# Two decayed-attention outputs feed two feed-forward layers: three places in the order of the side work are rewritten

## The chip, the cores and the metric

The kernel runs on one core of one Trainium2 chip. The metric is the device time of one execution in microseconds (us), as the median of three runs. Engines are named as in the profile: PE is TensorE (PEld its weight loads), DVE is VectorE, ACT is ScalarE, POOL is GpSimd, SP is SyncE, which here issues nearly all DMAs.

## The reference, cut to what matters

```python
# q, k, v: (4, 8, 576, 64), f: (4, 8, 576)
scores = q @ k^T / 8 + cumsum(log f)[i] - cumsum(log f)[j]      # causal
attn = softmax(scores);  x = attn @ v                           # x: (2304, 512)
h = x @ w_in;   x = (h * clip(h + 3, 0, 6) / 6) @ w_out         # w_in (512, 2048), w_out (2048, 512)
h = x @ w_in2;  x = (max(h, 0) + alpha * min(h, 0)) @ w_out2    # layer two, same shapes
```

All weights arrive as 64-bit numbers.

## The kernel before, in words

**Attention.** 32 heads in 16 pairs; every pair gives nine units of up to 128 rows. A head's raw data, q and k in one tile `rqk` of 128x1216 words, is requested by `load_head`. `prep_head` and `prep_low` (lines 296 to 317) make the two operands of the score product of it, and the decay's cumulated sums come in as four extra rows of each operand (`q2[64:68]`, `k2[64:68]`). For heads 0 and 1 these rows are built on the core. For all others they are written to DRAM once, as `ak_d` (line 502) and `aq_d` (line 517), and read back head by head (lines 295 and 296). The first unit of head 2 multiplies `k2` on line 347. Head 3's raw data is requested at line 518, behind both row stores; SP issues in program order.

**Feed-forward.** Tokens are three pairs p of 2 x 384, hidden features eight groups g of 256. A set (layer, g, p) multiplies a 2x2 block of the token pair with a 2x2 block of the group in seven products instead of eight (`product`, `PROD`), each of 2 x 3 matmuls, since an operand is kept as a rounded high part and a low part (the rest): high x high, high x x-low, weight-low x high. `SEQ` is the order of a set: products 1, 5, 6, 3, 7, 2, 4 (P1 to P7 in the text), with a `q` between them, one piece of the output product of the set before (`piece`). P1, P6, P7 and P4 accumulate in one bank hA, P5 and P3 in hC, P2 alone in hB; after P1, P6 and P5 ACT copies the bank away (`keep`, line 687), and after P3, P7 and P2 DVE adds the copy (`add`, line 690). P6 must not write hA before P1's copy is done, P7 not before P6's copy, P4 not before P7's sum, P3 not hC before P5's copy. `activate` makes g of each sum on ACT and DVE, then ACT rounds it (line 664) and POOL makes its low part (line 665). The first three pieces of the next set need the g of P7 first, and its low part with their third matmul.

**Slots.** Every character of `SEQ` is a slot. Work that is not PE's is hung on slots: `at` for what follows a product, `behind` for side work, and the table of numbers beside each name says in which slot it is written into its engine's stream. Engines run their streams in that order.

**Weights (side work).** `conv_ops` turns the raw words of a group into single precision: magnitude m (ACT), floor f, shift s, join j, sign g (DVE), for the four pieces 0 to 3 (0 and 1 are w_in). Out of pieces 0 (tile `wa`) and 1 (`wb`) POOL forms S1, S2 (in `wc`), S3 (in `wa`) and S4 (in `wb`), line 162. ACT then rounds the parts a, b, c, d (ha, hb, hc, hd, line 176), and POOL makes the low parts (la, lb, lc, ld, line 180). Part a holds the weights of P1 and P7 and is made of S3's tile `wa`, b those of P2 and P4, c those of P5 and P6 (tile `wc`), d that of P3, made of S4. In layer two a conversion for g+1 starts three slots into set (g, p=0) and is needed at set (g+1, p=0), 26 slots after that set's start; there are seven. `CONV_EVEN` is the table of these seven and of nothing else. m2 (the magnitude of piece 2) writes `wc` again, which S4 reads.

**Token blocks (side work).** `build_parts` forms the seven x blocks of a pair: sums (line 223), high parts on ACT (line 226), low parts (line 231) on POOL or DVE in turn. P1, P5, P6, P3, P7, P2, P4 use blocks 0, 3, 6, 2, 4, 1, 5. `build` with `even` spreads the list of `BUILD` in the order of its text evenly over slots: for pair 1 in layer one, from slot 1 of set (0, g=1, p=0) with 1.5 steps a slot, and for pair 0 of layer two, in a stretch of 51 slots in layer one's last third.

The lines that the steps touch:

```python
PROD = {1: (0, 0, "A"), 2: (2, 1, "B"), 6: (5, 6, "A"), 5: (4, 3, "C"), 7: (1, 4, "A"), 3: (6, 2, "C"),
        4: (3, 5, "A")}
SEQ = ("1qq5q6q3q7q2q4q", "1q5q6q3q7q2q4")
FIRST = ("152637..4", "15qq6qq3q7q2q4q", "1qq5qq6qq3q7q2q4q")
SUM = {"S1": (("S", 0), (0, 1), (1, 1), ALU.add), "S3": ((0, 1), (0, 0), (0, 1), ALU.subtract),
       "S2": (("S", 1), ("S", 0), (0, 0), ALU.subtract), "S4": ((1, 0), (1, 0), ("S", 1), ALU.subtract)}
```

Of the kernel before, what the change touches and what calls it, by code (L numbers as in the profile page):

```python
# [21 lines left out]
def decay_attention_ffn2_kernel(ctx, tc, qk, v, f, wi1, wo1, wi2, wo2, alpha, out):  # L22
# [24 lines left out]
    CONV_FIRST = "ho0 2 m3 2 lo0 3 f3 3 s3 4 j3 5 g3 6 ho1 8 lo1 9 wi0 30 wi1 33 wo0 36 wo1 38"  # L47
    CONV_A = "m0 0 f0 2 s0 3 j0 4 g0 5 m1 4 f1 6 s1 7 j1 8 g1 9"
    CONV_B = "hb 11 S1 11 S3 12 lb 13 S2 13 S4 14 ha 14 hc 16 la 16 hd 17 lc 18 ld 19 m2 19 f2 20 s2 21 j2 22 g2 23 m3 21 f3 24 s3 25 j3 26 g3 27 ho0 25 lo0 27 ho1 29 lo1 31 wi0 40 wi1 43 wo0 46 wo1 48"
    CONV_EVEN = "m0 0 f0 1 s0 2.5 j0 4 g0 5.5 m1 5 f1 7 s1 8.5 j1 10 g1 11.5 S1 12 S2 13 hc 14 S3 14 hb 15 lc 15 lb 16 ha 16 S4 17 m2 18 hd 18 f2 19 ld 19 s2 20 la 20 j2 21 m3 21 g2 22.5 f3 23 ho0 23 lo0 24 s3 24.5 j3 26 g3 27 ho1 28 lo1 29 wi0 40 wi1 43 wo0 46 wo1 48"  # L50
    CONV_TURN = "S1 11 S3 12 S2 13 hb 30 ha 30 hc 31 lb 32 la 33 S4 34 lc 35 m2 38 hd 37 ld 38 f2 41 s2 42 j2 43 g2 44 m3 42 f3 46 s3 47 j3 48 g3 49 ho0 47 lo0 49 ho1 51 lo1 52 wi0 58 wi1 61 wo0 64 wo1 66"
    BUILD = "h0 2 l0 4 a3 6 h3 9 l3 11 h2 9 l2 11 a4 13 a6 15 h4 16 l4 18 h1 17 l1 19 h6 19 l6 21 a5 22 h5 26 l5 28"
    early = {}
    ORD, QA, QB, QL = "TMEVDS", 3, 7, 2
# [163 lines left out]
    def build_parts(k, p, add, subs):  # L218

        turn = [0]  # L220

        def combine(d, a, b):
            add.tensor_sub(out=d, in0=a, in1=b)  # L223

        def high(b, c, x):
            nc.scalar.copy(out=XS[k][0][:, b, c], in_=x)  # L226

        def low(b, c, x):
            e = subs[turn[0] % len(subs)]
            turn[0] += 1  # L230
            e.tensor_sub(out=XS[k][1][:, b, c], in0=x, in1=XS[k][0][:, b, c].bitcast(F32))  # L231

        adds, highs, lows = {}, {}, {}
        for c in range(KH):
            b11, b12, b21, b22 = (place(p, j, n, c) for j in range(2) for n in range(2))
            for b, d, x, y in ((3, b11, b12, b11), (4, b12, b22, b12), (6, b22, b22, b11), (5, b21, b21, b22)):
                adds[b, c] = lambda a=(d, x, y): combine(*a)
            for b, x in ((0, b11), (1, b21), (2, b22), (6, b22), (3, b11), (4, b12), (5, b21)):
                highs[b, c] = lambda a=(b, c, x): high(*a)
                lows[b, c] = lambda a=(b, c, x): low(*a)  # L240
        return adds, highs, lows
# [18 lines left out]
    def attention():  # L260
        with ExitStack() as ax:
# [13 lines left out]
            def load_head(h):  # L275
                raw = rawp.tile([128, QW + S], F32, tag="raw", name="rqk")
                nc.sync.dma_start(out=raw, in_=qk[h])
                raws[h] = (raw[:, 0:QW], raw[:, QW:QW + S])
                if h % 2 == 0:
                    p = h // 2  # L280
                    vt = vp.tile([128, KT, 128], F32, tag="v", name="vt")
                    nc.sync.dma_start(out=vt, in_=v[p // NPAIR, p % NPAIR])
                    vs[p] = vt
# [8 lines left out]
            def prep_head(h):  # L292
                if h not in slots:
                    q1, q2, k1, k2 = op_tiles(h)
                    nc.sync.dma_start(out=q2[64:68].bitcast(F32), in_=aq_d[h % 2, h // 2])
                    nc.sync.dma_start(out=k2[64:68].bitcast(F32), in_=ak_d[h % 2, h // 2])
                q1, q2, k1, k2 = slots[h]
                rq, rk = raws[h]
                e = AS0[h] if h < 2 else AS
                scaled(e[0], q1, rq, SCALE)  # L300
                scaled(e[1], k1, rk)
                if h < 4:
                    scaled(e[2], k2[0:64], rk[0:64])
# [196 lines left out]
            load_head(2)  # L500
            for a in range(2):
                nc.sync.dma_start(out=ak_d[a, 0:NP], in_=ak[32 * a:32 * a + NP].bitcast(F32))
            prep_head(1)
            prep_low(1)
            nc.gpsimd.memset(three, 3.0)
# [9 lines left out]
                scaled("P", aq[ps, 0:2, t0:t0 + TAIL], hl[ps, :, 512:S].bitcast(F32))  # L515
            for a in range(2):
                nc.sync.dma_start(out=aq_d[a, 0:NP], in_=aq[32 * a:32 * a + NP].bitcast(F32))
            load_head(3)
            nc.gpsimd.tensor_scalar(out=alpha_sb, in0=alpha_sb, scalar1=-1.0, scalar2=None, op0=ALU.mult)
            px.close()  # L520
            ptp = ax.enter_context(tc.tile_pool(name="ptp", bufs=3, reuse_waits="tile"))
# [111 lines left out]
    def aside(d, fn):  # L633
        behind.setdefault(now[0] + int(d), []).append(fn)
# [104 lines left out]
    def side_work(s):  # L739

        ff, g, p = s

        def conversion(ops, text, keep, scale=1, shift=0, first=0, last=10 ** 6):
            for name, t in table(text, first, last):
                if keep or name[0] != "w":
                    aside(t * scale + shift, ops[name])

        def build(k, pair, subs, add=nc.vector, even=None):
            for i, (t, fn) in enumerate(build_ops(k, pair, add, subs)):
                aside(t if even is None else even[0] + i / even[1], fn)  # L750

        both = (nc.gpsimd, nc.gpsimd, nc.vector)
        if s == (0, 1, 0):
            conversion(early["first"], CONV_FIRST, True)
            build(1, 1, both, even=(1, 1.5))
        if s == (0, 0, 1):
            ops = conv_ops(0, 2)
            conversion(ops, CONV_A, True, 1, 1)
            conversion(ops, CONV_B, True, 1, 4, 0, 25)
            conversion(ops, CONV_B, True, 1, 7, 25)  # L760
        if p == 0 and (1 if ff else 2) <= g + 1 < NG and not (ff == 0 and g < 2):
            ops, keep = conv_ops(ff, g + 1), g + 1 < NG - 2
            for text in ((CONV_EVEN,) if ff else (CONV_A, CONV_B)):
                conversion(ops, text, keep, 1, 3 if ff else 5)
        if p == NPR - 1:
            order = gorder[ff][1]
            j = order.index(g)
            if j >= 2:
                load_w(ff, g, 1)
            if 1 <= j < NG - 1:  # L770
                load_w(ff, order[j + 1], 0)
            if ff == 0 and j == 1:
                build(1, 0, (nc.gpsimd,), nc.gpsimd, (0, 0.7))
            if ff == 0 and j == NG - 3:
# [106 lines left out]
```

## Time and profile before

| | |
|---|---|
| runs | 1023.65, 1024.52, 1025.59 us; median 1024.52 |
| the profiled execution | 1023.57 us, of which the span of instructions is 1021.8 |
| its mean granted clock of PE | 0.992 |
| busy share: DVE, ACT, POOL | 72%, 58%, 58% |
| chain that ended last: PE, DVE, POOL, ACT | 71%, 15%, 5%, 4% |
| DMA moved | 139.18 MB, mean 136 GB/s |

The profile was taken of one execution. In its timeline a row is a start, a duration, the engine, the line and the operation, out<-in, the shape, how many in a row are merged (x), and in brackets how long the engine was idle before it and what released it. A row's duration holds the instruction's own latency, so rows of PE overlap. In the list of waits each row gives an engine and line, what it waited for, the total, how often, and the longest.

### The profile page before, as it was taken

Reading aid. Unit: us, or ns where it says so; the run is one execution under the profiler, and the core shown is the slowest. Engines: PE = TensorE matmul, PEld = TensorE weight load, DVE = VectorE, ACT = ScalarE, POOL = GpSimd, SP = SyncE. Lnnn points to the kernel's source line nnn. Section 1 sums busy time; section 2 is a strip of 40 time slices with the busy share of each in tenths; the row PEclk is TensorE's granted clock in tenths of the full one; section 3 lists DMA queues with packets and bytes.
Section 4 is the critical chain, followed back from the end, with each engine's and each line's share of the span. In section 5 each row is a group of like instructions: output and inputs, shape, how many; then the busy total and the mean of one; then the engine's idle time right before and its main releaser. Section 6 shows DMA issues by size and latency. Waiting matters only on the chain.

```text
span 1021.8 us, 15850 instructions
## 1 busy us (share of the span) xinstructions
PE 966.4 (95%) x5488; PEld 862.7 (84%) x5488; DVE 739.2 (72%) x1284; ACT 588.5 (58%) x1444; POOL 589.0 (58%) x577
## 2 busy tenths in 40 slices
PE   4999999998999999999999997999999999999998
PEld 3666666678899999998999996888888888888987
DVE  6787987857688788878345668677887778735454
ACT  4677787776555555554544354766555556564452
POOL 7467578856655656566555377565556556532221
PEclk9899999999999999999999998999999999999999
DMA  7555576501424444210254513344244420244531
GB/s 206 178 173 153 173 241 212 149 6 42 155 71 169 181 171 181 94 43 1 76 223 179 203 53 104 131 166 175 85 174 163 167 83 0 94 170 160 226 144 73
DMA packets 32260, 139.18 MB, mean 136 GB/s; under 512 B 4156, under 2 KB 4156, under 8 KB 29044
## 3 DMA queue, kind: packets, MB, share of 16 engines
q1 hardware_dynamic: 32176, 138.17, 39.0%
q8 instruction: 43, 0.70, 0.3%
q14 instruction: 37, 0.30, 0.1%
q10 hardware_dynamic: 4, 0.00, 0.0%
HBM read 94.06 MB, written 39.94 MB: 131 GB/s over the span
## 4 chain that ended last, share of the span: by engine, by line
PE 71%; DVE 15%; POOL 5%; ACT 4%; issue 3%; DMA 1%; SPq 1%; ACTq 0%; DVEq 0%; POOLq 0%
PE o L715 17%; PE o L713 16%; PE hA L682 16%; PE hC L682 9%; PE pv L436 4%; PE hB L682 4%; DVE nm L323 3%; PE tp L379 2%; PE sc L346 2%; POOL wi L180 2%; POOL g L665 1%; DVE nm L325 1%; DVE r L223 1%; ACT g L664 1%; PE sc L347 1%
## 5 line engine op out<-in xcount | busy, mean ns | idle before, releaser
L682 PE MATMUL hA<-xh,wi 128*128 128x384 f32 x768 | 227.1, 341 | 22.2 <-POOL wi L180 11.2
L713 PE MATMUL o<-g,wo 128*128 128x384 f32 x1152 | 232.3, 340 | 1.2 <-POOL g L665 1.2
L715 PE MATMUL o<-wo,g 128*128 128x512 f32 x864 | 224.1, 395 | 1.8 <-POOL g L665 1.4
L665 POOL TENSOR_TENSOR g<-t,g 128x384 fp32r<-128x384 f32 x120 | 127.7, 1065 | 162.2 <-ACT g L664 142.5
L713 PEld LDWEIGHTS o<-g,wo 128*128 128x128 f32 x1152 | 205.8, 189 | 2.1 <-POOL g L665 1.8
L715 PEld LDWEIGHTS o<-wo,g 128*128 128x128 f32 x864 | 160.5, 188 | 29.0 <-POOL g L665 2.7
L682 PEld LDWEIGHTS hA<-xh,wi 128*128 128x128 f32 x768 | 142.1, 189 | 29.8 <-POOL wi L180 13.5
L665 POOL TENSOR_TENSOR g<-s,g 128x384 fp32r<-128x384 f32 x72 | 75.8, 1053 | 155.3 <-ACT g L664 144.9
L733 DVE TENSOR_TENSOR r<-o,r 128x512 f32<-128x512 f32 x126 | 86.5, 687 | 64.0 <-PE o L715 62.9
L682 PE MATMUL hA<-xl,wi 128*128 128x384 f32 x384 | 130.4, 340 | 2.1 <-POOL xl L231 2.1
L722 DVE SCALAR_TENSOR_TENSOR r<-o,r 128x384 f32<-128x384 f32 x168 | 91.4, 551 | 50.5 <-PE o L713 50.1
L664 ACT CAST g<-t 128x384 fp32r<-128x384 f32 x120 | 61.7, 514 | 107.4 <-DVE t L656 89.2
L682 PE MATMUL hC<-xh,wi 128*128 128x384 f32 x384 | 114.3, 338 | 1.3 <-ACT s L687 1.3
L331 ACT ACTIVATE p<-sc,nm 128x128 f32<-128x128 f32 (+4 forms) x160 | 84.5, 531 | 21.3 <-DVE nm L325 9.9
L323 DVE TENSOR_REDUCE nm<-sc 128x1 f32<-128x128 f32 (+4 forms) x160 | 71.5, 469 | 10.5 <-PE sc L348 7.8
L231 POOL TENSOR_TENSOR xl<-r,xh 128x384 fp32r<-128x384 f32 x65 | 74.8, 1168 | 5.1 <-ACT xh L226 4.9
L682 PEld LDWEIGHTS hA<-xl,wi 128*128 128x128 f32 x384 | 72.7, 189 | 5.4 <-POOL xl L231 2.3
L664 ACT CAST g<-s 128x384 fp32r<-128x384 f32 x72 | 37.0, 514 | 65.9 <-DVE s L659 65.1
L682 PEld LDWEIGHTS hC<-xh,wi 128*128 128x128 f32 x384 | 71.1, 188 | 3.8 <-ACT s L687 1.6
L687 ACT COPY s<-hA 128x384 f32<-128x384 f32 x96 | 45.9, 478 | 44.3 <-PE hA L682 44.2
L379 PE MATMUL tp<-ident,p 128*128 128x128 f32 x384 | 69.4, 285 | 0.6 <-ACT pt L395 0.6
L346 PE MATMUL sc<-k,q 128*128 128x256 f32 (+2 forms) x128 | 55.9, 437 | 11.6 <-DVE k L314 9.4
(128 smaller groups left out, 1927.2 us busy)
## 6 DMA issues: line engine op xcount, KB each, us to landing
wid<-wi SPq DMA_DIRECT2D x24, 896.0 KB
wi<-wid SPq DMA_DIRECT2D x12, 1792.0 KB
rqk<-in_qk SPq DMA_DIRECT2D x32, 608.0 KB
raw<-in_wi SPq DMA_DIRECT2D x32, 512.0 KB
raw<-in_wo SPq DMA_DIRECT2D x32, 512.0 KB
wod<-wo SPq DMA_DIRECT2D x24, 512.0 KB
wo<-wod SPq DMA_DIRECT2D x12, 1024.0 KB
vt<-in_v SPq DMA_DIRECT2D x16, 320.0 KB
```

Of the source, the lines that this page charges most:

```text
L231: e.tensor_sub(out=XS[k][1][:, b, c], in0=x, in1=XS[k][0][:, b, c].bitcast(F32))
L323: nc.vector.tensor_reduce(out=nm[:, i:i + 1], in_=src, axis=AX.X, op=ALU.max, negate=True)
L331: nc.scalar.activation(out=pt[:, c0:c0 + cw], in_=src, func=AF.Exp, bias=nm[:, 0:1], scale=1.0, accum_out=dsts[i])
L346: nc.tensor.matmul(out=sc[:, 0:n], lhsT=q1[:, qs], rhs=k1[:, 0:n], start=True, stop=False)
L379: nc.tensor.transpose(tp[:, j, :], pt[:, 128 * j:128 * j + 128], ident)
L664: nc.scalar.copy(out=gt[n][i][:, 0], in_=hold["g"])
L665: nc.gpsimd.tensor_sub(out=gt[n][i][:, 1], in0=hold["g"], in1=gt[n][i][:, 0].bitcast(F32))
L682: nc.tensor.matmul(out=h, lhsT=a, rhs=b[:, x, kc], start=new and kc + e == 0, stop=kc == KH - 1 and e == 2, skip_group_check=not new)
L713: nc.tensor.matmul(out=o[:, 0:NB], lhsT=a[:, cs], rhs=b, start=st, stop=sp)
L715: nc.tensor.matmul(out=o, lhsT=b[:, cs], rhs=a, start=st, stop=sp)
L722: later(0, lambda: nc.vector.scalar_tensor_tensor(out=acc, in0=o[:, 0:NB], scalar=1.0 / 6.0, in1=acc, op0=ALU.mult, op1=ALU.add))
L733: nc.vector.tensor_add(out=acc, in0=o, in1=acc)
```

## The change

Three edits. In `CONV_EVEN` part a's rounding and low part move ahead of part b's, and the steps of pieces 0 and 1 and of the sums are written up to 1.5 slots earlier. `build` with `even` takes its order from a new list, `BUILD_FIRST`, in which block 6 (P6's) stands ahead of blocks 4 and 1. `load_head(3)` moves from behind the `aq_d` stores to between the `ak_d` and the `aq_d` stores.

```diff
-    CONV_EVEN = "m0 0 f0 1 s0 2.5 j0 4 g0 5.5 m1 5 f1 7 s1 8.5 j1 10 g1 11.5 S1 12 S2 13 hc 14 S3 14 hb 15 lc 15 lb 16 ha 16 S4 17 m2 18 hd 18 f2 19 ld 19 s2 20 la 20 j2 21 ...
+    CONV_EVEN = "m0 0 f0 1 s0 2 j0 3.5 g0 5 m1 4 f1 6.5 s1 8 j1 9 g1 10 S1 11 S2 12 S3 12 hc 13 ha 13 lc 14 hb 14 la 15 lb 16 S4 17 m2 18 hd 18 f2 19 ld 19 s2 20 j2 21 ...
+    BUILD_FIRST = "h0 l0 a3 h3 l3 h2 l2 a4 a6 h6 l6 h4 l4 h1 l1 a5 h5 l5"
     BUILD = "h0 2 l0 4 a3 6 h3 9 l3 11 h2 9 l2 11 a4 13 a6 15 h4 16 l4 18 h1 17 l1 19 h6 19 l6 21 a5 22 h5 26 l5 28"
...
-    def build_ops(k, p, add, subs):
+    def build_ops(k, p, add, subs, even=None):
         adds, highs, lows = build_parts(k, p, add, subs)
+        if even is not None:
+            fns = [{"h": highs, "l": lows, "a": adds}[name[0]][int(name[1]), c]
+                   for name in BUILD_FIRST.split() for c in range(KH)]
+            return [(even[0] + i / even[1], fn) for i, fn in enumerate(fns)]
...
             for a in range(2):
                 nc.sync.dma_start(out=ak_d[a, 0:NP], in_=ak[32 * a:32 * a + NP].bitcast(F32))
+            load_head(3)
             prep_head(1)
...
                 nc.sync.dma_start(out=aq_d[a, 0:NP], in_=aq[32 * a:32 * a + NP].bitcast(F32))
-            load_head(3)
...
-            for i, (t, fn) in enumerate(build_ops(k, pair, add, subs)):
-                aside(t if even is None else even[0] + i / even[1], fn)
+            for t, fn in build_ops(k, pair, add, subs, even):
+                aside(t, fn)
```

The changed kernel's lines lie up to five numbers higher. Each of the following pieces shows the stream before first and the changed one second.

POOL in one conversion of layer two: the three L162 rows are S1, S2, S3, the first L180 (of `wc`) is lc, that of `wb` with 2x256 is lb, that of `wa` is la, the fourth L162 is S4, and the L180 of 2x128 is ld; the L665 rows are the low parts of g.

```order
L162 TENSOR_TENSOR wc<-wa,wb 128x2x128
L162 TENSOR_TENSOR wc<-wc,wa 128x2x128
L162 TENSOR_TENSOR wa<-wa 128x2x128
L180 TENSOR_TENSOR wi<-wc,wi 128x2x256
L180 TENSOR_TENSOR wi<-wb,wi 128x2x256
L162 TENSOR_TENSOR wb<-wb,wc 128x2x128
L665 TENSOR_TENSOR g_8310<-s,g_8310 128x384
L180 TENSOR_TENSOR wi<-wb,wi 128x2x128
L665 TENSOR_TENSOR g_8338<-s,g_8338 128x384
L180 TENSOR_TENSOR wi<-wa,wi 128x2x256
```

```order
L163 TENSOR_TENSOR wc<-wa,wb 128x2x128
L163 TENSOR_TENSOR wc<-wc,wa 128x2x128
L163 TENSOR_TENSOR wa<-wa 128x2x128
L181 TENSOR_TENSOR wi<-wc,wi 128x2x256
L181 TENSOR_TENSOR wi<-wa,wi 128x2x256
L181 TENSOR_TENSOR wi<-wb,wi 128x2x256
L163 TENSOR_TENSOR wb<-wb,wc 128x2x128
L670 TENSOR_TENSOR g_8311<-s,g_8311 128x384
L181 TENSOR_TENSOR wi<-wb,wi 128x2x128
L670 TENSOR_TENSOR g_8339<-s,g_8339 128x384
```

la, which stood behind the second g of the set (P7's), now stands ahead of lb, S4, ld and both g.

ACT in the first of the seven conversions, set (layer two, g=0, p=1): L687 of hA is first P1's copy and, further down, P6's, L687 of hC is P5's, L731 moves output pieces out, and the L176 rows are hc, hb and ha of `wc`, `wb` and `wa`.

```order
L687 COPY s<-hA 128x384
L731 COPY r_80<-o 128x512
L687 COPY s<-hC 128x384
L176 CAST wi<-wc 128x2x256
L731 COPY r_80<-o 128x512
L176 CAST wi<-wb 128x2x256
L687 COPY s<-hA 128x384
L176 CAST wi<-wa 128x2x256
```

```order
L692 COPY s<-hA 128x384
L736 COPY r_80<-o 128x512
L177 CAST wi<-wc 128x2x256
L177 CAST wi<-wa 128x2x256
L692 COPY s<-hC 128x384
L177 CAST wi<-wb 128x2x256
L736 COPY r_80<-o 128x512
L692 COPY s<-hA 128x384
```

Here P5's copy now stands behind hc and ha. In the six later conversions hc and ha stand behind P5's copy and ahead of P6's, where all three roundings stood behind both.

SP at the start of the kernel: the first L277 row is head 2's raw data, the L502 and L517 rows the row stores, the L114 rows two raw weight pieces, and L295 and L296 the rows of head 2 read back.

```order
L277 DMA rqk<-in_qk 128x1216
L282 DMA vt<-in_v 128x640
L502 DMA ak_d<-ak 16x2304 x2
L517 DMA aq_d<-aq 16x2560 x2
L277 DMA rqk<-in_qk 128x1216
L114 DMA raw<-in_wi 128x512 x2
L295 DMA q_275<-aq_d 4x640
L296 DMA k_277<-ak_d 4x576
```

```order
L282 DMA rqk<-in_qk 128x1216
L287 DMA vt<-in_v 128x640
L507 DMA ak_d<-ak 16x2304 x2
L282 DMA rqk<-in_qk 128x1216
L523 DMA aq_d<-aq 16x2560 x2
L115 DMA raw<-in_wi 128x512 x2
L300 DMA q_275<-aq_d 4x640
L301 DMA k_277<-ak_d 4x576
```

Head 3's 128x1216 words now stand ahead of the `aq_d` stores; what follows the stores keeps its order. The edit of the block list leaves every stream's rows alike in operation and shape; only which block a row works on changes.

## Rows read from the trace of the kernel before

**Rows 1.** The page, busy time and share of the span
```profile
PE 966.4 (95%) x5488; PEld 862.7 (84%) x5488; DVE 739.2 (72%) x1284; ACT 588.5 (58%) x1444; POOL 589.0 (58%) x577
```
**Rows 2.** Waits of PE: total us, times, longest
```profile
PE hA L682 <- POOL wi L180: 11.2, 7, 1.9
...
PE sc L347 <- DMA k<-ak_d: 5.3, 1, 5.3
...
PE hA L682 <- POOL xl L231: 2.1, 1, 2.1
```
**Rows 3.** Timeline of POOL, a conversion of layer two (start us, us)
```profile
704.20 0.73 POOL L162 TENSOR_TENSOR wc<-wa,wb 128x256 f32<-128x256 f32 x1 [0.69 <-DVE wb L148]
...
706.48 1.30 POOL L180 TENSOR_TENSOR wi<-wc,wi 128x512 fp32r<-128x512 f32 x1
...
709.11 1.09 POOL L162 TENSOR_TENSOR wb<-wb,wc 128x256 f32<-128x256 f32 x1
...
713.56 1.02 POOL L665 TENSOR_TENSOR g<-s,g 128x384 fp32r<-128x384 f32 x1 [1.49 <-ACT g L664]
714.54 1.71 POOL L180 TENSOR_TENSOR wi<-wa,wi 128x512 fp32r<-128x512 f32 x1
```
**Rows 4.** Timeline of PE, same stretch: P7, the next set's P1, its first piece
```profile
708.18 0.34 PE L682 MATMUL hA<-xh,wi 128*128 128x384 f32 x1
...
716.30 0.61 PE L682 MATMUL hA<-xh,wi 128*128 128x384 f32 x2 [1.64 <-POOL wi L180]
...
717.10 1.56 PE L715 MATMUL o<-wo,g 128*128 128x512 f32 x6
```
**Rows 5.** Timeline of ACT, same stretch: P6's copy and m2
```profile
704.59 0.48 ACT L687 COPY s<-hA 128x384 f32<-128x384 f32 x1 [1.86 <-PE hA L682]
...
710.23 0.67 ACT L132 ACTIVATE wc<-raw 128x512 f32<-128x512 f32 x1
```
**Rows 6.** Timeline of DVE, same stretch: the step before g of P7 and P2
```profile
712.27 0.60 DVE L659 SCALAR_TENSOR_TENSOR s<-t,alpha_sb,s 128x384 f32<-128x384 f32 x1
...
715.05 1.61 DVE L659 SCALAR_TENSOR_TENSOR s<-t,alpha_sb,s 128x384 f32<-128x384 f32 x1
```
**Rows 7.** Timeline of the first of the seven conversions: ACT, POOL, PE
```profile
635.39 0.49 ACT L687 COPY s<-hC 128x384 f32<-128x384 f32 x1
...
637.80 0.74 POOL L162 TENSOR_TENSOR wa<-wa 128x256 f32<-128x256 f32 x1
...
637.90 0.34 PE L682 MATMUL hC<-xh,wi 128*128 128x384 f32 x1
...
647.96 0.62 PE L682 MATMUL hA<-xh,wi 128*128 128x384 f32 x2 [1.14 <-POOL wi L180]
```
**Rows 8.** Timeline around P6 of set (0,0,1), and that stretch's granted clock
```profile
254.51 3.76 POOL L231 TENSOR_TENSOR xl<-r,xh 128x384 fp32r<-128x384 f32 x3
...
258.32 0.62 PE L682 MATMUL hA<-xl,wi 128*128 128x384 f32 x1 [2.09 <-POOL xl L231]
...
258.40:261.80 3.40, 3.40 (x11) 3.40 (x12) 2.84 (x6) 1.31 (x3) 0.52 (x1) 0.50 0.00 0
...
262.10 0.56 DVE L722 SCALAR_TENSOR_TENSOR r<-o,r 128x384 f32<-128x384 f32 x1 [0.82 <-PE o L713]
...
268.86 1.02 POOL L665 TENSOR_TENSOR g<-t,g 128x384 fp32r<-128x384 f32 x1 [1.04 <-ACT g L664]
...
270.30 2.27 PE L713 MATMUL o<-g,wo 128*128 128x384 f32 x12
```
**Rows 9.** Timeline of SP's queue at the start; windows: DMA share and GB/s stand last
```profile
15.01 0.90 SPq L517 DMA_DIRECT2D aq_d<-aq  x2
16.01 1.46 SPq L277 DMA_DIRECT2D rqk<-in_qk  x1
...
12.00:16.00 4.00, 4.00 (x17) 3.02 (x17) 2.91 (x7) 2.25 (x8) 3.56 (x11) 1.00 1.02 304
16.00:20.00 4.00, 4.00 (x22) 3.14 (x22) 2.40 (x6) 2.25 (x10) 3.68 (x4) 1.00 0.90 135
```

More of the change, by code (lines that the diff above doesn't have):

```diff
@@ L49, in decay_attention_ffn2_kernel @@
     CONV_B = "hb 11 S1 11 S3 12 lb 13 S2 13 S4 14 ha 14 hc 16 la 16 hd 17 lc 18 ld 19 m2 19 f2 20 s2 21 j2 22 g2 23 m3 21 f3 24 s3 25 j3 26 g3 27 ho0 25 lo0 27 ho1 29 lo1 31 wi0 40 wi1 43 wo0 46 wo1 48"
-    CONV_EVEN = "m0 0 f0 1 s0 2.5 j0 4 g0 5.5 m1 5 f1 7 s1 8.5 j1 10 g1 11.5 S1 12 S2 13 hc 14 S3 14 hb 15 lc 15 lb 16 ha 16 S4 17 m2 18 hd 18 f2 19 ld 19 s2 20 la 20 j2 21 m3 21 g2 22.5 f3 23 ho0 23 lo0 24 s3 24.5 j3 26 g3 27 ho1 28 lo1 29 wi0 40 wi1 43 wo0 46 wo1 48"
+    CONV_EVEN = "m0 0 f0 1 s0 2 j0 3.5 g0 5 m1 4 f1 6.5 s1 8 j1 9 g1 10 S1 11 S2 12 S3 12 hc 13 ha 13 lc 14 hb 14 la 15 lb 16 S4 17 m2 18 hd 18 f2 19 ld 19 s2 20 j2 21 m3 21 g2 22.5 f3 23 ho0 23 lo0 24 s3 24.5 j3 26 g3 27 ho1 28 lo1 29 wi0 40 wi1 43 wo0 46 wo1 48"
     CONV_TURN = "S1 11 S3 12 S2 13 hb 30 ha 30 hc 31 lb 32 la 33 S4 34 lc 35 m2 38 hd 37 ld 38 f2 41 s2 42 j2 43 g2 44 m3 42 f3 46 s3 47 j3 48 g3 49 ho0 47 lo0 49 ho1 51 lo1 52 wi0 58 wi1 61 wo0 64 wo1 66"
+    BUILD_FIRST = "h0 l0 a3 h3 l3 h2 l2 a4 a6 h6 l6 h4 l4 h1 l1 a5 h5 l5"
     BUILD = "h0 2 l0 4 a3 6 h3 9 l3 11 h2 9 l2 11 a4 13 a6 15 h4 16 l4 18 h1 17 l1 19 h6 19 l6 21 a5 22 h5 26 l5 28"
```

## The prediction

> **What bounds the kernel now.** I read the page first: PE is busy 95% of the span, every other engine 72% or less [rows 1]. So the time is PE's work plus its gaps, and an edit that adds no matmul can only fill or open gaps. Next I read the list of PE's waits, where the reader is to see three entries, one for each edit [rows 2]: bank hA's first matmul waits for a low part of weights seven times, 11.2 us in all; a score product waits once, 5.3, for the rows of `ak_d`; and hA waits once, 2.1, for a block's low part. Then I read the timelines at these places, engine by engine, to find how much earlier the awaited thing could come and what is late next.
>
> **Edit 1, the order of the conversion.** The seven waits are P1 of a new group waiting for la, the low part of its weights. The reason is POOL's order, not POOL's load: la starts at 714.54, right behind the low part of P7's g, and that one had waited 1.49 for ACT [rows 3]. P1 starts at 716.30 after 1.64 of waiting, so it was ready at 714.66 [rows 4]. In the changed order la stands right behind lc, which ends at 706.48 + 1.30 = 707.78; at 1.30 to 1.71, the two durations that such a part has here [rows 3], la ends at 709.1 to 709.5. That is 5 us before P1 wants it. Of the total of 11.2 the first wait is 1.14 [rows 7], the six others are 10.1: **−10.1** for these six.
>
> What is late next at these boundaries? The first piece follows P1, and its third matmul takes the low part of P7's g. The piece starts at 717.10 and its six matmuls take 1.56 [rows 4], so the third is wanted at 717.10 − 1.64 + 2 x 0.26 = 716.0. The low part ends at 713.56 + 1.02 = 714.58 [rows 3]: 1.4 to spare, if it does not move. POOL's idle 1.49 before it takes up the inserted la of 1.71 but for 0.2. I count nothing for it, and come back to it as a rival.
>
> ACT is the second engine with a new order. In the six later conversions hc and ha stand ahead of P6's copy, now at 704.59 [rows 5], and ha needs S3. Even with S1 where it is, at 704.20, three sums of about 0.75 end at 706.45, just before lc [rows 3]; a rounding as long as a copy, 0.48, and the copy itself then end at 707.5, and P7, which needs that copy, starts at 708.18 [rows 4]. As the sign step ahead of S1 is also written 1.5 slots earlier, S1 should come sooner than this. I count nothing.
>
> The first conversion starts three slots later in its set, so there P5's copy is the one that falls behind hc and ha. It runs at 635.39 now. S3 is at 637.80 and ends at 638.54; POOL cannot do it much earlier, since S1 is behind a low part of g. With ha at about 0.5 and the copy at 0.49 the bank is free at 639.6, while P3, which writes it, starts at 637.90 [rows 7]: a new wait of about 1.8, against 1.1 won at the end of that set. **+0.7**. No trace shows this wait, so I bound it: −1.1 if S3 comes early enough; and +2.4 if the wait also halves PE's clock. What halving costs I take from the stretch behind the block's wait, 3.40 us at a granted clock of 0.50 [rows 8], 1.2 instead of 2.4 GHz, so 3.40 x 0.5 = 1.7. I take the middle: behind the boundary's wait of 1.64, six matmuls of 512 columns took 1.56 [rows 4], which is full pace, so a wait of 1.8 need not halve it.
>
> **Edit 2, head 3's raw data.** The request moves from behind the `aq_d` stores, issued at 15.01, to ahead of them; it was at 16.01 [rows 9]. It is 128 x 1216 x 4 = 622,592 bytes. The rows of head 2, read back behind the stores, are what PE waits 5.3 for [rows 2], and they still stand behind the same total of bytes: head 3 and two raw weight pieces. From 12 to 16 the DMA engines moved 304 GB/s, from 16 to 20 only 135, at 0.90 busy: the stores are small pieces and slow [rows 9]. If big packets fill that slow stretch, the most to be won is what the slow stretch lost, 4 x (1 − 135/304) = 2.2. If instead the stores land later by the whole of head 3's data, and the reads with them, it costs 622,592 B / 304 GB/s = 2.0. Engines that are 0.90 busy have little to fill; the total is the same either way. I take a small gain, **−0.5**, nearest the busy share (0.10 of the 4 us idle, 0.4).
>
> **Edit 3, block 6 ahead of blocks 4 and 1.** P6 of set (0,0,1) waits 2.09 for the last of a run of three low parts, 3.76 from 254.51, and then runs 3.40 at clock 0.50 [rows 8]. Now block 6's part is the first of that run, ready at 254.51 + 3.76/3 = 255.8; P6 is ready at 258.32 − 2.09 = 256.2. Wait and clock are both gone: 2.1 + 1.7 = 3.8 at this place. But blocks 4 and 1 feed P7 and P2 later, and the DVE work behind, P7's sum and g, can only come as much earlier as DVE now waits for PE, 0.82 at 262.10. So the low part of that g, now at 268.86 for 1.02, ends at best at 269.06. The piece that takes it starts at 270.30 and its third matmul is at 270.30 + 2 x 2.27/12 = 270.65, so the gain that survives there is 270.65 − 269.06 = **−1.6** [rows 8]. Bounds: −3.8 if DVE follows fully, and +0.1 if the wait of 2.2 that appears at the piece halves the clock in its turn (1.7). The same list orders the stretch of 51 slots for layer two's first pair; PE's list has a single wait for a block's low part [rows 2], the one above, so I cost that use at nothing; if its blocks 4 or 1 came too late there, it would show as such a wait.
>
> **Sum.** −10.1 + 0.7 − 0.5 − 1.6 = −11.5. The profiled execution took 1023.57, so 1012.1; it lay 0.95 under the median of the three runs, which puts the forecast at **1013.0**. The bounds together: −10.1 − 1.1 − 2.2 − 3.8 = −17.2 and −10.1 + 2.4 + 2.0 + 0.1 = −5.6, or 1007.3 to 1018.9; not all fall the same way.
>
> **Rivals.**
>
> *The gains of edits 2 and 3 come whole* (−3.8 and −2.2 in place of −1.6 and −0.5): 1013.0 − 3.9 = 1009.1. For it speaks that DVE is busy only 72% [rows 1]; against it the 0.82. Chance 0.12.
>
> *The stores land behind head 3's data*: +2.0 in place of −0.5, 1015.5. For it: the engines are already 0.90 busy when the stores are issued [rows 9]; against: the bytes ahead of the read rows are the same. Chance 0.10. The Trainium skill (DMA: Bandwidth & Descriptors, section "Queues, rings and completion order") says that each DMA engine takes descriptors in the order of the ring, which speaks against issuing head 3 first; no row here shows one engine's order.
>
> *POOL's unbroken run makes S4 late.* lc, la and lb now run one after the other beside DVE. If each takes 1.71, as la did, S4 ends at 706.48 + 3 x 1.71 + 1.09 = 712.7 instead of 710.2 [rows 3]. m2 on ACT, which follows S4 at once, at 710.23 [rows 5], moves with it, and if ACT's rounding of g behind m2 moves too, the low part of g ends 2.5 later, at 717.1, where 716.0 is wanted: 1.1 at six boundaries, 6.6 back: 1019.6. For it: la took 1.71 beside a DVE step that took 1.61 and not 0.60 [rows 3, 6]; against: ACT is 58% busy [rows 1] and has room to catch up. Chance 0.13. The Trainium skill (SBUF — State Buffer, section "Who interferes with whom") says that a DVE step with two SBUF inputs and a GpSimd step that reads SBUF contend for one port pair; the long pair of rows agrees.
>
> *Slower: the same chain goes through DVE as well.* The step of P7's g on DVE, 0.60 at 712.27, becomes 1.61 like its neighbour [rows 6], because a moved low part lies beside it. The low part of g ends at 718.1, 2.1 late, at all seven boundaries: +14.7, so 1027.7. It decides from 11.5/7 = 1.6 of wait, that is when the low part ends 3.1 later than its 714.58. Against: both delays must add up at each boundary. Chance 0.04.
>
> *The change doesn't do what it says*: each boundary wait is replaced one for one by the one for g's low part, which stood just before la on POOL. Then −10.1 becomes 0 and the other terms, −1.4, leave 1023.1. Against: the 1.4 to spare. Chance 0.03.
>
> **How the numbers follow.** The forecast has the rest, 0.58. A difference under 0.2%, 2 us, can't be told from none. The four cases at 1019.6 and below hold 0.93; the slow end of the POOL case reaches no change with 0.03, so faster 0.90, same 0.06, slower 0.04. The range 1009.0 to 1018.5 leaves out most of the POOL case, the no-effect and slower cases, and a little of the low end, together 0.2.
>
> **What would show it.** In the changed profile PE's waits of hA for a low part of weights are gone, and la on POOL ends 4 to 5 us before P1. Near 638 a wait of hC for ACT's copy, about 1.8, is new; if it is absent, the term is −1.1. Near 258 hA no longer waits for a block and the granted clock stays 1.00; instead a piece near 270 waits for the low part of g, or P7 waits for DVE. The wait for `ak_d` stands at 4.8, at 3.1 or at 7.3 in the three cases of edit 2. A new entry "o waits for POOL's g" at the seven boundaries, about 1 each, would show the POOL case; 2 each, with the DVE step at 1.61, the slower one. The forecast is wrong if such entries sum to more than 5 us, or if waits that I costed at nothing (P7 for P6's copy) appear in the six later conversions.

## The result and the profile after

The changed kernel takes 1014.52 us (median of 4 runs, 1013.06 to 1015.60), against 1024.52. The ratio is 0.9901, 95% interval 0.9884 to 0.9918: 10.1 us faster, between 8.4 and 11.9. The profiled execution took 1013.06 with a span of 1011.3, against 1023.57 and 1021.8, so the two traces differ by 10.5.

The page and the waits of PE, in the views of [rows 1, 2]. The lines of the changed kernel lie five numbers higher there (L682 is now L687, L715 is L720, L180 is L181).

```profile
PE 968.2 (96%) x5488; PEld 861.2 (85%) x5488; DVE 740.6 (73%) x1284; ACT 589.2 (58%) x1444; POOL 585.2 (58%) x577
```
```profile
PE o L720 <- POOL g L670: 3.2, 7, 0.7
...
PE sc L352 <- DMA k<-ak_d: 1.5, 1, 1.5
PE hA L687 <- ACT g L669: 1.4, 1, 1.4
```

The seven waits for POOL's `wi`, 11.2, are gone, and so is the one for a block. The wait for `ak_d` went from 5.3 to 1.5. Three things are to be seen beside this: waits of o for POOL's g grew from 1.4 us in three waits to 3.2 in seven, hA waits 1.4 at a new place, and the busy time of PE grew by 1.8, although its instructions are the same. Short waits are in that busy time, as part of a row that merges several matmuls.

So I compare starts instead of waits. The two streams of PE are the same 5,488 matmuls in the same order; the table gives the start of the same matmul in both traces, and other starts named below are compared in the same way.

| matmul | before | after | difference |
|---|---|---|---|
| first one with head 2's rows | 26.63 | 25.82 | −0.8 |
| pair 1 | 33.01 | 29.30 | −3.7 |
| set (0,0,1), the first of P6 | 255.79 | 252.85 | −2.9 |
| its P3 | 261.90 | 254.95 | −7.0 |
| its next piece, with P7's g | 270.64 | 266.25 | −4.4 |
| layer turn, P1 | 626.63 | 622.91 | −3.7 |
| first conversion, P3 | 637.90 | 635.20 | −2.7 |
| P1 with la, group 1 | 647.96 | 644.05 | −3.9 |
| P1 with la, group 2 | 682.87 | 676.63 | −6.2 |
| P1 with la, group 3 | 716.30 | 708.52 | −7.8 |
| a piece in the middle of group 3 | 733.34 | 726.30 | −7.0 |
| P1 with la, group 4 | 749.76 | 741.00 | −8.8 |
| P1 with la, group 7 | 850.10 | 838.49 | −11.6 |
| a piece in the middle of group 7 | 867.74 | 857.19 | −10.6 |

From group 1 to group 7 the six boundaries, each counted with the first piece behind it, give 10.6: 2.2 at the first, about 1.7 at each of the others. But in the middle of the groups part of it is lost again: 0.4 in group 2, 0.7 in each of groups 3 to 6 and 0.95 in group 7, together 4.2. The start gives 3.7 (0.8 of it is lost again up to P6, where a stretch at half clock lies at 243), and edit 3 gives 4.0 at P6 and takes back 2.6; another 0.7 is lost by the layer turn.

**The start.** The transfers, as [rows 9], and the granted clock behind the wait, first of before, then of after (windows; clock, DMA share and GB/s stand last).

```profile
26.40:33.00 6.60, 6.37 (x27) 5.38 (x28) 3.44 (x10) 3.37 (x11) 4.21 (x5) 0.50 0.58 201
```
```profile
16.00:20.00 4.00, 3.93 (x19) 3.19 (x18) 3.01 (x5) 1.59 (x6) 3.26 (x4) 1.00 1.00 273
...
24.40:33.00 8.60, 7.18 (x59) 5.87 (x60) 6.17 (x17) 7.15 (x26) 4.08 (x5) 1.00 0.57 190
```

From 16 to 20 the DMA engines now move 273 GB/s where it was 135, so head 3's packets do fill the slow stretch of the stores. Head 2's rows are there 0.8 earlier. The rest of the shorter wait (1.5 for 5.3) is no gain: the last matmul ahead of it starts at 23.80 where it was 20.95, so PE comes later. (In the eight other profiled kernels with this edit it starts at 20.2 to 22.6, so that lateness does not belong to the edit.) The gain is behind the wait, where PE stays at full clock; in the kernel before it ran at 0.50 until 33.

**A group boundary in layer two**, as [rows 3, 4, 5] (timelines of POOL, ACT and PE; idle time and its releaser in brackets).

```profile
701.85 1.30 POOL L181 TENSOR_TENSOR wi<-wa,wi 128x512 fp32r<-128x512 f32 x1
703.12 1.29 POOL L181 TENSOR_TENSOR wi<-wb,wi 128x512 fp32r<-128x512 f32 x1
704.49 0.94 POOL L163 TENSOR_TENSOR wb<-wb,wc 128x256 f32<-128x256 f32 x1
...
708.75 1.01 POOL L670 TENSOR_TENSOR g<-s,g 128x384 fp32r<-128x384 f32 x1 [1.36 <-ACT g L669]
```
```profile
705.46 0.68 ACT L133 ACTIVATE wc<-raw 128x512 f32<-128x512 f32 x1
```
```profile
708.52 0.51 PE L687 MATMUL hA<-xh,wi 128*128 128x384 f32 x2
...
709.23 1.78 PE L720 MATMUL o<-wo,g 128*128 128x512 f32 x6
```

la ends at 703.15, 5.4 ahead of the matmul that takes it (708.52). But the low part of P7's g ends at 709.76, and the first piece, which takes it with its third matmul, lasts 1.78 instead of the 1.56 of [rows 4]: it waits about 0.2. There is no slack left here, where I had counted 1.4.

**The middle of a group.** The piece 17.8 us behind the boundary is the first that takes g of P7 in the group's next set. The rows that it waits for: DVE's f1 (L136), P7's activation step on DVE (L664), ACT's rounding, POOL's low part, PE.

```profile
723.38 0.65 DVE L136 TENSOR_SCALAR wb<-wb 128x512 f32<-128x512 f32 x1
...
723.95 0.61 DVE L664 SCALAR_TENSOR_TENSOR s<-t,alpha_sb,s 128x384 f32<-128x384 f32 x1
...
724.65 0.51 ACT L669 CAST g<-s 128x384 fp32r<-128x384 f32 x1 [1.26 <-DVE s L664]
...
725.24 1.01 POOL L670 TENSOR_TENSOR g<-s,g 128x384 fp32r<-128x384 f32 x1 [1.49 <-ACT g L669]
...
726.30 1.19 PE L720 MATMUL o<-wo,g 128*128 128x512 f32 x4 [0.36 <-POOL g L670]
```

POOL's low part ends at 726.25 and the piece goes on at 726.30. The bracket shows 0.36, but the same piece took 1.56 before, and now from 725.22 to 727.49: 0.7 longer. The gap in the list shows only half of what this wait cost; the starts show all of it.

**Edit 3.** DVE between P6 and P4 of set (0,0,1), as [rows 8], and PE's two waits there. L695 is the sum of P3 (hC) and of P7 (hA); L144, L149 and L136 are conversion steps.

```profile
256.60 0.68 DVE L144 SCALAR_TENSOR_TENSOR wa<-raw,wa 128x512 uint32<-128x512 uint32 x1
257.31 1.39 DVE L149 SCALAR_TENSOR_TENSOR wa<-raw,wa 128x512 uint32<-128x512 uint32 x1
...
259.10 0.77 DVE L136 TENSOR_SCALAR wb<-wb 128x512 f32<-128x512 f32 x1
259.79 0.55 DVE L695 TENSOR_TENSOR s<-hC,s 128x384 f32<-128x384 f32 x1
...
262.12 0.55 DVE L695 TENSOR_TENSOR s<-hA,s 128x384 f32<-128x384 f32 x1
```
```profile
262.82 0.41 PE L687 MATMUL hA<-xh,wi 128*128 128x384 f32 x1 [1.41 <-ACT g L669]
...
266.25 2.03 PE L718 MATMUL o<-g,wo 128*128 128x384 f32 x10 [0.47 <-POOL g L670]
```

DVE is unbroken. The first of the two lines of PE is P4, which may write hA only when P7's sum has read it; the sum ends at 262.67, so the wait is for DVE, although the list names ACT; ACT's rounding of g does not touch this bank. The second is the piece with the low part of P7's g.

### The profile page after: what moved, and what is told of

It reads as the page before. It is cut to its first block, busy times and chain, and to the rows that moved or that the text cites. A ratio compares the mean times of both kernels' runs of the same rounds, so it can differ in the third digit from the quotient of the medians.

```text
span 1011.3 us, 15842 instructions
## 1 busy us (share of the span) xinstructions
PE 968.2 (96%) x5488; PEld 861.2 (85%) x5488; DVE 740.6 (73%) x1284; ACT 589.2 (58%) x1444; POOL 585.2 (58%) x577
## 4 chain that ended last, share of the span: by engine, by line
PE 51%; DVE 28%; ACT 8%; POOL 7%; issue 5%; DMA 2%; SPq 0%; POOLq 0%; DVEq 0%; ACTq 0%
PE o L718 15%; PE hA L687 11%; PE o L720 7%; PE hC L687 6%; PE pv L441 4%; POOL wi L181 3%; DVE nm L328 3%; PE hB L687 3%; DVE r L738 2%; DVE s L664 2%; DVE s L695 2%; PE tp L384 2%; ACT g L669 2%; PE sc L351 1%; DVE wb L144 1%
## 5 line engine op out<-in xcount | busy, mean ns | idle before, releaser
L687 PE MATMUL hA<-xh,wi 128*128 128x384 f32 x768 | 226.9, 341 | 12.6 <-DVE s L695 8.1
L720 PE MATMUL o<-wo,g 128*128 128x512 f32 x864 | 227.1, 396 | 4.1 <-POOL g L670 3.2
L720 PEld LDWEIGHTS o<-wo,g 128*128 128x128 f32 x864 | 159.2, 188 | 35.5 <-POOL g L670 8.8
L687 PEld LDWEIGHTS hA<-xh,wi 128*128 128x128 f32 x768 | 143.1, 190 | 17.9 <-DVE s L695 8.7
L687 PE MATMUL hA<-xl,wi 128*128 128x384 f32 x384 | 130.6, 340 | 0.0
L687 PE MATMUL hC<-xh,wi 128*128 128x384 f32 x384 | 114.3, 338 | 1.4 <-ACT s L692 1.3
L687 PEld LDWEIGHTS hA<-xl,wi 128*128 128x128 f32 x384 | 73.0, 190 | 3.2
L687 PEld LDWEIGHTS hC<-xh,wi 128*128 128x128 f32 x384 | 70.9, 188 | 4.2 <-ACT s L692 2.1
L351 PE MATMUL sc<-k,q 128*128 128x256 f32 (+2 forms) x128 | 55.6, 435 | 13.1 <-DVE k L319 10.1
L687 PE MATMUL hC<-xl,wi 128*128 128x384 f32 x192 | 64.8, 338 | 0.0
```

The source lines that it names most:

```text
L351: nc.tensor.matmul(out=sc[:, 0:n], lhsT=q1[:, qs], rhs=k1[:, 0:n], start=True, stop=False)
L687: nc.tensor.matmul(out=h, lhsT=a, rhs=b[:, x, kc], start=new and kc + e == 0, stop=kc == KH - 1 and e == 2, skip_group_check=not new)
L720: nc.tensor.matmul(out=o, lhsT=b[:, cs], rhs=a, start=st, stop=sp)
```

## The experiments

Each run is compared with the kernel before on the same chip. Gains are (1 − ratio) x 1024.5, with the interval in brackets.

**The edits one at a time.** The first kernel has the changed `CONV_EVEN` line alone, the second only this:

```diff
+            load_head(3)
             prep_head(1)
...
-            load_head(3)
```

and the third only `BUILD_FIRST` and the code that reads it.

> The kernel before with the new CONV_EVEN alone. Theory: the seven waits of hA for POOL's low part go (-10.2 at the six later boundaries, -1.1 at the first), and about 4 us come back at pieces 17 us behind the boundaries, where o waits for POOL's low part of g because f1 now stands ahead of the activation's step on DVE: 1017 to 1018.5. In the first conversion the clock's slow stretch should lie as in the kernel before, so a wait of hC for ACT's copy of up to 1.8 can show there; if it stays under 0.3, S1 to S3 came early enough by the order alone. Rival (the waits are replaced one for one): above 1022. Rival (nothing comes back, what is missing in the whole change comes from the other edits): 1013 to 1014.5.

Measured: 1018.00, ratio 0.9936 (0.9919 to 0.9953), 6.6 us faster (4.8 to 8.3). The theory's range. The first conversion shows the new wait that I had forecast, but smaller (timelines of ACT and PE; L176 of `wa` is ha, then P5's copy, then P3):

```profile
639.14 0.62 ACT L176 CAST wi<-wa 128x512 fp32r<-128x512 f32 x1
639.66 0.47 ACT L687 COPY s<-hC 128x384 f32<-128x384 f32 x1
```
```profile
640.19 0.44 PE L682 MATMUL hC<-xh,wi 128*128 128x384 f32 x1 [0.34 <-ACT s L687]
```

The start of P3 moved by 0.6 against the matmuls ahead of it, where I had 1.8.

> The kernel before with load_head(3) alone moved. Theory: the rows of head 2 land about 0.8 earlier and PE's clock does not fall behind the shortened wait, together -3.3: 1021.2, with no stretch of granted clock 0.5 between 26 and 33. Rival (the prediction's: only the landing counts): -0.5, 1024.0, with the slow stretch still there. Rival (the 3.3 belong to one lucky profile): several executions spread over 1021 to 1025.

Measured: 1023.17 (12 runs, 1019.50 to 1024.57), ratio 0.9984 (0.9972 to 0.9995): 1.6 us faster (0.5 to 2.9). Between the first two expectations, and the third is true as well: single executions spread over 5 us, and the profile of the changed kernel was a lucky one. It waited 1.5 for the rows; the other eight profiled kernels with this edit waited 3.3 to 4.8, the three without it 5.1 to 5.8. The transfers do not spread so: from 16 to 20 the DMA engines moved 257 to 318 GB/s in all nine with the edit, and 127 to 144 in the three without. Those three all ran about 6.8 us at clock 0.50 behind the wait; with the edit it is between none and 6.8:

```profile
26.90:30.20 3.30, 3.30 (x16) 2.78 (x15) 2.36 (x7) 2.43 (x8) 2.22 (x4) 0.50 0.56 214
30.30:33.00 2.70, 2.70 (x26) 2.10 (x25) 2.35 (x5) 1.71 (x8) 2.61 (x3) 1.00 0.44 79
```

That is this run (windows, clock third from the end), which came back to full clock at 30.3.

> The kernel before with BUILD_FIRST alone. Theory: the wait of P6 for block 6 (2.1) and the slow stretch behind it go, and P7's sum and g, which DVE cannot bring forward, take back most: -0.8 to -1.6, 1023.0 to 1023.7. Rival (the slow stretch of 3.4 us that the changed kernel has at 243 is not from this edit): without it -2.5 to -3.0, 1021.5 to 1022. If the slow stretch is at 246 here too, it comes from this edit, or lies where it falls by chance.

Measured: 1023.22, ratio 0.9991 (0.9980 to 1.0002): 0.9 faster (−0.2 to 2.0), in the theory's range and not clearly apart from nothing. P6 does not wait, no slow stretch lies near it, and 1.95 and 0.46 come back:

```profile
266.88 0.41 PE L687 MATMUL hA<-xh,wi 128*128 128x384 f32 x1 [1.95 <-ACT g L669]
270.30 0.97 PE L718 MATMUL o<-g,wo 128*128 128x384 f32 x4 [0.46 <-POOL g L670]
```

What makes the clock fall near 243 to 261 stays open: the profiled kernels have none, one or two stretches of 3.4 us there, behind waits of 1.9 to 2.1 us. One wait of 2.1 near 245 is in all twelve profiles, and six of them have a stretch at half clock behind it. Of edit 3 more can be said: the three kernels with the old block order all have such a stretch at or just behind P6's wait, and of the nine with the new order none has one there. The three gains add up to 9.1, against 10.1 for all; the intervals are too wide to say whether 1.0 comes from the edits together.

**The two halves of edit 1.** Inside `CONV_EVEN` the change moves la ahead and it moves the steps up (S3 by two slots, the others by up to 1.5). In each of these kernels, made from the changed one, one half is undone.

```diff
-"m0 0 f0 1 s0 2 j0 3.5 g0 5 m1 4 f1 6.5 s1 8 j1 9 g1 10 S1 11 S2 12 S3 12 hc 13 ha 13 lc 14 hb 14 la 15 lb 16 ...
+"m0 0 f0 1 s0 2.5 j0 4 g0 5.5 m1 5 f1 7 s1 8.5 j1 10 g1 11.5 S1 12 S2 13 hc 14 S3 14 ha 15 lc 15 hb 16 la 16 lb 16 ...
```

> The changed kernel with the steps m0 to S3 at the slots of the kernel before, and only the order of roundings and low parts new (ha, la ahead of hb, lb). Theory (POOL's order is all that the boundary waits need, the earlier steps only crowd DVE): no wait of hA for a low part of weights, and no more wait of o for g's low part than with f1 put back: 1011.5 to 1013. Rival (the early steps are needed: with S1 to S3 at their old place the longer run lc, la, lb, S4 pushes the low part of P7's g): waits of o for POOL's g of 0.5 to 1 at each boundary, 1016 to 1019.

Measured: 1020.45, ratio 0.9959 (0.9947 to 0.9972), 4.2 faster. The rival is right. hA waits for no low part of weights any more, but o waits twice in each group, at the boundary and in the middle:

```profile
PE o L720 <- POOL g L670: 5.7, 14, 0.7
PE o L720 <- ACT g L669: 1.7, 6, 0.5
```

The chain at a boundary (POOL's S4 and low part of P7's g, ACT's m2, PE's first piece):

```profile
741.63 0.74 POOL L163 TENSOR_TENSOR wb<-wb,wc 128x256 f32<-128x256 f32 x1
...
745.68 1.01 POOL L670 TENSOR_TENSOR g<-s,g 128x384 fp32r<-128x384 f32 x1 [1.43 <-ACT g L669]
```
```profile
742.40 0.68 ACT L133 ACTIVATE wc<-raw 128x512 f32<-128x512 f32 x1 [1.41 <-POOL wb L163]
```
```profile
746.75 1.20 PE L720 MATMUL o<-wo,g 128*128 128x512 f32 x4 [0.35 <-POOL g L670]
```

m2 waits for S4 and stands on ACT ahead of what makes P7's g. From the end of S4 to the start of g's low part it is 3.36 in the kernel before [rows 3], 3.32 in the changed one and 3.31 here: a chain of fixed length. Against the matmul that takes la (with the wait taken out in the kernel before, 714.66), S4 ends 4.5 ahead before, 3.1 ahead in the changed kernel, and 2.3 ahead here (744.62 − 742.37). The inserted la moves S4 back by more than 2, the early steps win 0.8 of it, and that is about what PE waits here.

```diff
-... hc 13 ha 13 lc 14 hb 14 la 15 lb 16 S4 17 m2 18 hd 18 f2 19 ld 19 s2 20 j2 21 ...
+... hc 13 lc 14 hb 14 lb 16 ha 16 S4 17 m2 18 hd 18 f2 19 ld 19 s2 20 la 20 j2 21 ...
```

> The changed kernel with the order of roundings and low parts of the kernel before (la behind g again, at slot 20; hb, lb ahead of ha), all steps ahead of them staying early. Theory: the boundary waits of 1.65 return whole, 10 in all, and nothing is won by early steps: 1021.5 to 1022.5. Rival (la was late because all steps ahead of it were late): at least half of the gain stays, 1018 or less.

Measured: 1020.23, ratio 0.9958 (0.9945 to 0.9970), 4.3 faster. The waits are back, though the time is 1.3 below the theory's range:

```profile
PE hA L687 <- POOL wi L181: 9.6, 6, 1.7
```

Six of the seven waits, that is: at the first boundary, where the kernel before waits 1.14, the wait is gone, and 1.0 of this kernel's gain in the trace lies there.

Over the 2.5 that edits 2 and 3 gave alone, one half wins 1.7 and the other 1.8; both together win 7.6.

**What comes back in the middle of a group.** On DVE, f1 stands ahead of P7's activation step (an expectation below says P3's; the rows shown above are P7's), and s0 (L140) ahead of P3's sum (L695 of hC). In the kernel before f1 stood behind P7's step, but s0 already stood where it is now. DVE in the middle of group 3, before and after:

```profile
724.21 1.26 DVE L139 TENSOR_SCALAR wa<-wa 128x512 uint32<-128x512 uint32 x1
725.40 0.55 DVE L690 TENSOR_TENSOR s<-hC,s 128x384 f32<-128x384 f32 x1
```
```profile
718.11 1.46 DVE L140 TENSOR_SCALAR wa<-wa 128x512 uint32<-128x512 uint32 x1
...
719.48 0.54 DVE L695 TENSOR_TENSOR s<-hC,s 128x384 f32<-128x384 f32 x1
```

The changed kernel with f1 back, with s0 later, and with both (there also ha at slot 14, behind P5's and P6's copies on ACT):

```diff
-... f1 6.5 ...
+... f1 7 ...
```

> The changed kernel with f1 of CONV_EVEN written at slot 7 again (6.5 in the change), so that on DVE the activation's step and the sum of P2 stand ahead of f1. Theory: the waits of o for POOL's low part of g 17 us behind five boundaries, 0.36 in the list and 0.73 in PE's pace, go: -3.7 against the changed kernel, 1010.8. Rival (PE is 1.7 earlier there and DVE, ACT and POOL simply do not follow, whatever the place of f1, as in the last group, which has no conversion and loses 1.05 too): within 1 us of the changed kernel, 1013.5 to 1015.

Measured: 1012.76, ratio 0.9889 (0.9872 to 0.9905). Half of the theory: in groups 4 to 6 the piece loses 0.3 where it lost 0.7, and the last group loses its 0.95 as ever. The wait of hC in the first conversion is 0.84 here.

```diff
-... s0 2 ...
+... s0 3 ...
```

> The changed kernel with s0 alone at slot 3 (f1 stays at 6.5). Theory (two DVE orders share what comes back behind each boundary, 0.73: f1 ahead of P3's activation step made 0.3 of it, s0 ahead of P3's sum the rest): the waits of o for POOL's g 17 us behind the boundaries shrink from 0.73 to 0.2 to 0.4 each, 1012 to 1013. Rival (the sum of P3 starts a chain and its place alone decides): as with both, 1011 or less. Rival (f1 alone decides): as the changed kernel, 1014.5.

Measured: 1012.55, ratio 0.9883 (0.9865 to 0.9900); in groups 4 to 6 the piece loses 0.33 to 0.38. As expected, each makes about half.

> The changed kernel with f1 at slot 7, s0 at slot 3 and ha at slot 14, so that on DVE the sum of P3 stands ahead of s0 and the sum of P2 ahead of f1, and on ACT P5's and P6's copies stand ahead of ha. Theory (the order on DVE sets what comes back): the 0.4 that f1 alone left behind each boundary goes, and so does the wait of hC in the first conversion (0.84 with f1 back): 2 to 2.5 under f1 back's 1012.8, 1010.5. Rival (DVE is full from the boundary on, whatever its order): within 0.6 of 1012.8.

Measured: 1010.34, ratio 0.9864 (0.9849 to 0.9879). The theory is right: the first of the six boundaries gives 2.2, the five others 1.90 to 1.92 each, and nothing comes back in groups 2 to 6. The order on DVE, and the piece in one run of 1.56:

```profile
718.08 0.55 DVE L695 TENSOR_TENSOR s<-hC,s 128x384 f32<-128x384 f32 x1
718.54 1.00 DVE L140 TENSOR_SCALAR wa<-wa 128x512 uint32<-128x512 uint32 x1
...
723.68 0.54 DVE L695 TENSOR_TENSOR s<-hB,s 128x384 f32<-128x384 f32 x1
724.14 0.41 DVE L136 TENSOR_SCALAR wb<-wb 128x512 f32<-128x512 f32 x1
```
```profile
725.94 1.56 PE L720 MATMUL o<-wo,g 128*128 128x512 f32 x6
```

DVE has not one instruction less here; only their order is another. Its busy time is 734.5 where it was 740.6, since some steps last less long in their new places (s0 1.00 where it was 1.46, see the last section). What the move of ha gives beside the two others was not run by itself. The wait of hC is gone in this profile (in the next one it is 0.41).

**The last group.** As the kernel above, and

```diff
-            build(1 if ff else 0, 2, both)
+            build(1 if ff else 0, 2, both, shift=1 if ff else 0)
...
-                aside(t, fn)
+                aside(t + shift, fn)
```

> As the kernel with s0 and f1 behind the sums, and in layer two's last group the block of pair 2 is built one slot later, so that ACT rounds g ahead of the four roundings of the block. Theory (the 1.05 lost there is those four roundings, 1.74, standing ahead of g's): 1.0 under the kernel with s0 and f1 behind the sums. Rival (the block is then late and the next set's P1 waits for it): no gain, or up to 1 slower.

Measured: 1008.98, ratio 0.9846 (0.9833 to 0.9860), 15.8 faster than the kernel before (14.3 to 17.1): **the fastest kernel of this study**, and 5.5 below the changed one. ACT now rounds g ahead of the block's four roundings (L227):

```profile
852.08 0.51 ACT L669 CAST g<-s 128x384 fp32r<-128x384 f32 x1 [0.74 <-DVE s L664]
852.50 1.75 ACT L227 CAST xh<-r 128x384 fp32r<-128x384 f32 x4
```

The gain of 1.4 over the kernel above is near the 1.0 expected, but their intervals overlap. In the two traces PE wins 1.5 at this place, at the pieces that take this g.

**DVE behind edit 3.** On top of that kernel:

```diff
-            conversion(ops, CONV_A, True, 1, 1)
+            conversion(ops, CONV_A, True, 1, 5)
```

> The kernel with s0 and f1 behind the sums and the last group's block later, and in set (0,0,1) the conversion steps f0 to g1 of group 2 written four slots later, so that DVE makes the sums of P3 and P7 ahead of most of them. Theory (block 6 ahead gains 3.7 at P6 and gives back 1.4 to 2 at P4 and 0.5 at the next piece only because DVE does these steps first): the waits of hA for P7's sum near 265 and of o near 269 go, 1.5 to 2.4 under that kernel's 1009.0, 1007. Rival (the block parts on POOL or ACT hold P7 and P4 as well): less than 0.5 gained. Rival (the later steps make the weights of group 2 late): slower by the wait that then stands at set (0,2,0).

Measured: 1009.86, ratio 0.9851 (0.9836 to 0.9866): no gain that can be told. In the trace the mechanism shows: P4 does not wait for P7's sum any more. But the pieces behind it wait, the first of them newly, the second as before (0.47 in the kernel that this one was made from):

```profile
266.75 0.62 PE L718 MATMUL o<-g,wo 128*128 128x384 f32 x2 [0.33 <-ACT g L669]
267.88 2.02 PE L718 MATMUL o<-g,wo 128*128 128x384 f32 x10 [0.50 <-POOL g L670]
```

Against the kernel that it was made from, PE is 0.8 earlier behind this place, less than the 1.5 of the theory. DVE's order held P4; what holds g there was not tried further.

## Why the prediction was right, and where it was not

The forecast was 1013.0 and the measured time 1014.52; 11.5 were to be won and 10.1 were. Its terms fit less well than their sum, and that the sum came so near is in part luck: edit 1 gave 2.8 less than forecast, edit 2 gave 1.1 more.

| term | predicted | edit alone |
|---|---|---|
| edit 1, boundaries and first conversion | −9.4 | −6.6 (−8.3 to −4.8) |
| edit 2 | −0.5 | −1.6 (−2.9 to −0.5) |
| edit 3 | −1.6 | −0.9 (−2.0 to 0.2) |

**Edit 1, the boundaries.** "The six others are 10.1" is right: they gave 10.6 in the trace. The step that failed is "what is late next": the 1.4 to spare. I took POOL's idle 1.49 ahead of g's low part as room for la. It was no room, but the end of a chain from S4 over m2 on ACT; la, put ahead of S4, moved the whole chain. This was my rival of POOL's unbroken run, which I gave 0.13: its path was the right one, and its size, 1.1 at each boundary, is about 0.9 in the kernel without early steps (0.7 at the first of the six). Its price for the low parts was too high: la and lb took 1.30 and 1.29 in the changed kernel, where the rival had 1.71. I had also costed the early steps at nothing; they are what covers the chain.

**What I did not see**: the 4.2 that comes back in the middle of groups 2 to 7. A wait of 1.6 at the boundary had been a pause for DVE, ACT and POOL as well, and the next thing to be late was a whole set further, not at the boundary. The kernel without early steps bears this out: s0 and f1 stand on DVE in the order of the kernel before, which loses nothing there, and yet 0.75 to 0.8 is lost in the middle of groups 3 to 6. So f1's new place is only a part of it: with the pause gone, an order that cost nothing costs time, s0 ahead of P3's sum among it. I looked for the next late instruction only around the wait.

**The first conversion.** Predicted 1.8 of new wait (its own rows add up to 638.54 + 0.5 + 0.49 − 637.90 = 1.6) and +0.7. In the trace of edit 1 alone P3 lost 0.6, and P1 and the first piece behind it won 1.3 and 0.3: −1.0. "POOL cannot do it much earlier" failed. S3, which ha needs, started 0.1 ahead of P3 before (637.80 and 637.90, [rows 7]); in the changed kernel it starts 1.8 ahead:

```profile
633.38 0.74 POOL L163 TENSOR_TENSOR wa<-wa 128x256 f32<-128x256 f32 x1
```
```profile
635.20 0.44 PE L687 MATMUL hC<-xh,wi 128*128 128x384 f32 x1
```

Of these 1.7, 1.0 is PE's own lateness behind the layer turn (−3.7 at the layer turn, −2.7 at P3 in the table): 0.8 of it because PE spends 5.6 us behind the turn at a granted clock of 0.50 where it was 3.8, and 0.2 at P3 itself. The other 0.7 is POOL, which was not held as I had thought.

**Edit 2.** The mechanism held (big packets fill the stores' slow stretch, 273 GB/s for 135), the size did not. The 0.10 of idle time that I took was the wrong measure: engines that were 0.90 busy with the stores' small pieces took twice the bytes when head 3's packets were among them. And I left the clock out of this term, though I priced it for edit 3. The Trainium skill (DMA: Bandwidth & Descriptors, section "Queues, rings and completion order") has an engine take descriptors in the order of the ring; no row here shows that order. The rival that it stood beside, rows 2.0 later, is not borne out, since the rows came 0.8 earlier.

**Edit 3.** Right in path, and in the traces in sign: 4.0 won at P6 and most of it returned through DVE (its time alone can't be told from nothing). I had the place half right: I expected the wait at the piece, and 1.4 to 2.0 of it stands at P4, for P7's sum, with only 0.5 at the piece. The 1.4 are in profiles in which PE had come through the half clock near 245 and was later, the 2.0 in those in which it had not.

## What to carry to other kernels

A wait that is removed is also a pause that other engines lose: look for the next late instruction a whole period further on, not only around the wait. An idle time with a releaser in brackets is room only if what it waits for does not itself hang on the work you put ahead of it; follow the chain back before spending it. When two halves of an edit each win little (1.7 and 1.8 here), try them together (7.6), and then try the order on the next-busiest engine: moving two steps behind two sums on DVE, and a rounding behind two copies on ACT, won 3.8 us more than the change, without an instruction less.

## What the runs showed of the hardware

The same single-input step of DVE (L140) took 0.42 in one place and 1.45 in another, both in the kernel with f1 back; the long one started 0.12 behind a low part of POOL that lasted 1.29:

```profile
741.68 0.42 DVE L140 TENSOR_SCALAR wc<-wc 128x512 uint32<-128x512 uint32 x1
...
751.35 1.45 DVE L140 TENSOR_SCALAR wa<-wa 128x512 uint32<-128x512 uint32 x1
```
```profile
751.23 1.29 POOL L181 TENSOR_TENSOR wo<-wb,wo 128x512 fp32r<-128x512 f32 x1 [2.01 <-ACT wo L177]
```

The Trainium skill (SBUF — State Buffer, section "Who interferes with whom") says that a DVE step of this kind can enter a mode in which it contends with POOL for one port pair, and that the one that comes second waits for the whole instruction of the other. The two rows agree. No run varied it by itself, but the 64 steps of this line in this profile do: the 35 that start while POOL is at an instruction all end 0.28 to 0.29 behind the end of that instruction, however long it still had, and so last 0.65 to 1.48; the 29 others last 0.36 to 0.43, also those during which POOL starts something. The eleven other profiles show the same (0.28 to 0.32 behind the end, and 0.36 to 0.43). So a step's place on DVE also sets how long it lasts.

The first score product starts anywhere from 9.4 to 11.4 in the profiled kernels, whose code up to there is the same; a term of the start that is smaller than this can't be read from one profile.
